# Rolling the first head into loops on VectorE and ScalarE, and VectorE's later heads into nested loops

## Chip, cores, metric

One core of one Trainium2 chip. The metric is the device time of the kernel in microseconds (us), as the median of several runs. Where a ratio is given, it is the mean time of one kernel's runs over that of the other's of the same rounds (for the experiments it comes out when the run that was profiled is left out), so it is not quite the ratio of the medians that are quoted beside it.

## The reference, cut to what matters

A decode step for one token: attention over a long key-value cache, a small feed-forward part, and sums.

```python
B, Sq, D = 1, 1, 448
Hq, Hkv, Sk, Dh = 16, 8, 65536, 256
q = (x @ wq) ...                        # one token, 16 query heads, two per cache head
scores = q @ k^T * Dh ** -0.5           # k_cache, v_cache: 8 x 65536 x 256 bf16
p = softmax(scores); o = p @ v; attn = o @ wo
y = (silu(x @ w_gate) * (x @ w_up)) @ w_down * sigmoid(x @ w_r)
out = x + attn + xn + y
```

The two caches are 537 MB, and every byte is used once.

## The kernel before

Each cache head is cut into U = 4 units. A unit has 4 MB of K twice and 4 MB of V twice, which pass through a ring of four 4 MB slots. For K, TensorE transposes (as f32 pairs), VectorE evicts (copies out) three of four PSUM tiles and ScalarE one; then TensorE forms the scores. Sixteen such transposes with their scores are called a set. Part A is the first head's K, part B runs 28 turns with one head's V beside the next head's K, part C is the last head's V.

The loads are issued by SyncE in one straight sequence. A load waits until its slot is free; a V pair (8 MB, one load) waits for two slots:

```python
def pair_item(u):
    ...
    item(("v", u), [(ap..., A_v_cache[0, h]...[:, n0:n0 + 2 * CH, :], "slot%d" % s)],
         [("FREE", r + i - NSLOT) for i in range(2)])      # both slots must be free
# [cut]
for t in range(NT):
    slot_item("k", t + U, 0)
    pair_item(t)
    if t % U == 0:
        item(("wo", t // U), ...)
    slot_item("k", t + U, 1)
```

What each engine loops over is a table; the rest is unrolled:

```python
LOOPS = {"pe": {"A": 2, "B": 1, "C": 2}, "dve": {"B": U}, "act": {"B": U}}
```

TensorE (`pe`) thus already loops over pairs of units in A. VectorE (`dve`) and ScalarE (`act`) have A unrolled, and a loop of four turns in B.

## Time and profile before

| | before |
|---|---|
| first three runs | 1280.39, 1280.41, 1281.96 us |
| profiled span | 1279.0 us |
| busy: TensorE, VectorE, ScalarE | 77%, 46%, 36% |
| DMA | 549.0 MB, 429 GB/s, 99.7% of 16 engines |

From the profile's page of the kernel before: the head, the busy times (with share of the span and count), the DMA row of 40 slices, and the queue table:

```profile
span 1279.0 us, 23059 instructions
PE 984.8 (77%) x9859; PEld 674.4 (53%) x9859; DVE 584.2 (46%) x1091; ACT 459.6 (36%) x655; POOL 4.6 (0%) x35
DMA  9999999999999999999999999999999999999998
...
q1 hardware_dynamic: 18322, 549.04, 99.7%
...
q14 instruction: 6, 0.05, 0.0%
```

The DMA engines are the bound. No compute engine is near its limit, and the DMA row has no gap. The question for any change to compute is therefore only whether a load is issued later than the moment its queue runs dry.

The timeline around the end of the first pass of A (start, duration, engine, line, instruction; in brackets the idle time before and what ended it):

```profile
77.77 0.26 PE L372 MATMUL ps_s<-sel_bf,s 128*128 128x8 bf16 x4 [0.71 <-ACT s L450]
78.06 0.42 DVE L474 CAST S_sb<-ps_s 128x256 bf16<-128x256 f32 x1 [2.15 <-PE ps_s L372]
78.52 0.42 DVE L476 TENSOR_REDUCE m1p<-S_sb 128x2 f32<-128x256 bf16 x1
78.60 3.71 PE L372 MATMUL ps_t<-ident_f,ring 128*128 128x128 f32 x32 [0.58 <-issue]
79.70 3.68 DVE L426 COPY kt_buf<-ps_t 128x1024 bf16<-128x1024 bf16 x6 [0.77 <-PE ps_t L372]
```

The two loads, from SyncE's timeline, and the short chain ahead of the second one:

```profile
107.65 0.33 SPq L826 DMA_DIRECT2D ring<-in_A_v_cache_dram  x1
...
1231.79 2.01 SPq L826 DMA_DIRECT2D ring<-in_A_v_cache_dram  x2
```

```profile
1210.26 0.40 DVE L474 CAST S_sb<-ps_s 128x256 bf16<-128x256 f32 x1
1210.69 0.42 DVE L476 TENSOR_REDUCE m1p<-S_sb 128x2 f32<-128x256 bf16 x1
1211.15 0.16 DVE L480 TENSOR_REDUCE m<-m1p 128x2 f32<-128x8 f32 x1
1211.84 0.28 DVE L488 TENSOR_REDUCE gmax<-ps_m 2x1 f32<-2x128 f32 x1 [0.53 <-PE ps_o L372]
```

The first V pair starts to move at about 109.6 us, the late one at about 1233.6 us (counting bytes of packets in order), so both are issued only about 2 us ahead. Most other loads are issued 5 to 17 us ahead. I call these two the tight hand-overs.

### The profile page before, as it was taken

The numbers are of one execution on the slowest core, as the hardware profiler recorded it, in microseconds if no ns is written. First come the engines' busy times: TensorE is split into PE (matmuls) and PEld (weight loads), VectorE is DVE, ScalarE is ACT, GpSimd is POOL, SyncE is SP. The second block draws the span as 40 slices with busy tenths as digits, with TensorE's granted clock in tenths as the row PEclk, the third lists the DMA queues.
The fourth block names the chain that finished last, engine by engine and source line by source line (L and its number), as shares of the span: only waits on it lengthen the run. The fifth ranks groups of instructions, "written<-read, shape, count | busy, mean of one in ns | idle before, by whom it ended". The sixth has DMA issues, their size and how long they took to land.

```text
span 1279.0 us, 23059 instructions
## 1 busy us (share of the span) xinstructions
PE 984.8 (77%) x9859; PEld 674.4 (53%) x9859; DVE 584.2 (46%) x1091; ACT 459.6 (36%) x655; POOL 4.6 (0%) x35
## 2 busy tenths in 40 slices
PE   4998877778777787677786777877787876888754
PEld 3877554555554564445554545644455544556421
DVE  2676544454444554344543445543355443555310
ACT  1555433353333543234432244432334333344210
POOL 1000000000000000000000000000000000000000
PEclk9998888897878998888988889988799788899885
DMA  9999999999999999999999999999999999999998
GB/s 409 427 426 432 434 430 422 436 427 446 430 429 430 428 446 430 435 423 428 439 438 432 430 425 436 439 435 430 424 435 430 445 430 424 432 431 442 425 437 346
DMA packets 18342, 549.22 MB, mean 429 GB/s; under 512 B 1942, under 2 KB 3992, under 8 KB 5144
## 3 DMA queue, kind: packets, MB, share of 16 engines
q1 hardware_dynamic: 18322, 549.04, 99.7%
q8 instruction: 8, 0.13, 0.0%
q14 instruction: 6, 0.05, 0.0%
q10 hardware_dynamic: 6, 0.00, 0.0%
HBM read 549.03 MB, written 0.00 MB: 429 GB/s over the span
## 4 chain that ended last, share of the span: by engine, by line
DMA 65%; PE 33%; issue 1%; DVE 0%; SPq 0%; ACT 0%; ACTq 0%
DMA ring<-in_A_k_cache_dram 59%; PE ps_t L372 24%; PE ps_q L372 6%; DMA ring<-in_A_v_cache_dram 5%; PE ps_m L372 2%; PE ps_s L372 1%; DMA wr_row<-in_B_w_r_dram 0%; SPq L826 0%; ACT s L450 0%; DVE rowsf L340 0%; DVE xe_row L335 0%; DVE stat L312 0%; DVE rowsf L342 0%; DVE rowsf L319 0%; ACTq L826 0%
## 5 line engine op out<-in xcount | busy, mean ns | idle before, releaser
L372 PE MATMUL ps_t<-ident_f,ring 128*128 128x128 f32 x4096 | 546.7, 288 | 103.4 <-DMA ring<-in_A_k_cache_dram 82.6
L426 DVE COPY kt_buf<-ps_t 128x1024 bf16<-128x1024 bf16 x768 | 488.1, 684 | 268.0 <-PE ps_t L372 267.5
L372 PEld LDWEIGHTS ps_t<-ident_f,ring 128*128 128x128 f32 x4096 | 474.0, 147 | 211.3 <-issue 103.2
L428 ACT ACTIVATE kt_buf<-ps_t 128x1024 bf16<-128x1024 bf16 x256 | 262.2, 1024 | 242.8 <-PE ps_t L372 242.7
L372 PE MATMUL ps_o<-ring,p_sb 128*4 128x512 bf16 x2040 | 193.1, 545 | 144.5 <-DMA ring<-in_A_v_cache_dram 144.4
L450 ACT ACTIVATE s<-ps_q 98x512 bf16<-98x512 f32 x256 | 152.9, 597 | 273.5 <-PE ps_q L372 273.5
L372 PEld LDWEIGHTS ps_o<-ring,p_sb 128*4 128x4 bf16 x2040 | 55.7, 106 | 252.2 <-issue 233.5
L372 PE MATMUL ps_q<-kt_buf,q_cur 128*2 128x512 bf16 x2048 | 164.4, 398 | 0.0
L517 ACT ACTIVATE p_sb<-S_sb 128x128 bf16<-128x128 bf16 x64 | 19.0, 309 | 252.2 <-PE ps_o L372 249.2
L532 DVE RECIPROCAL rs<-ps_m 128x4 f32<-128x4 f32 x29 | 5.3, 182 | 226.5 <-PE ps_m L372 226.5
L372 PEld LDWEIGHTS ps_s<-sel_bf,s 128*128 128x128 bf16 x1024 | 59.9, 98 | 53.8 <-ACT s L450 50.8
L372 PE MATMUL ps_s<-sel_bf,s 128*128 128x8 bf16 x1024 | 63.9, 168 | 22.6 <-ACT s L450 22.6
L568 DVE CAST ob_sb<-ps_o 100x512 bf16<-100x512 f32 x29 | 20.1, 692 | 117.2 <-PE ps_o L372 117.2
L605 DVE TENSOR_TENSOR rowsf<-ps_m,rowsf 1x448 f32<-1x448 f32 x28 | 17.1, 612 | 53.9 <-PE ps_m L372 53.9
L372 PEld LDWEIGHTS ps_m<-rowsum,ones_f 128*128 128x128 f32 x116 | 21.6, 262 | 22.3 <-issue 22.3
L372 PEld LDWEIGHTS ps_q<-kt_buf,q_cur 128*2 128x2 bf16 x2048 | 27.1, 79 | 10.2 <-issue 5.0
L372 PE MATMUL ps_m<-wo_cur,oT_sb 128*1 128x448 bf16 x112 | 25.7, 352 | 0.0
L372 PE MATMUL ps_m<-rowsum,ones_f 128*128 128x2 f32 x116 | 24.0, 312 | 0.0
L372 PE MATMUL ps_m<-xnT_sb,w_area 128*128 x112 | 14.7, 184 | 2.8 <-issue 2.8
L372 PEld LDWEIGHTS ps_m<-wo_cur,oT_sb 128*1 128x1 bf16 x112 | 9.3, 83 | 13.5 <-issue 0.9
L474 DVE CAST S_sb<-ps_s 128x256 bf16<-128x256 f32 x32 | 12.9, 404 | 4.3 <-PE ps_s L372 4.3
L372 PEld LDWEIGHTS ps_m<-xnT_sb,w_area 128*128 x112 | 11.7, 104 | 5.8 <-issue 3.3
(87 smaller groups left out, 161.7 us busy)
## 6 DMA issues: line engine op xcount, KB each, us to landing
ring<-in_A_k_cache_dram SPq DMA_DIRECT2D x64, 4096.0 KB, 26.4
ring<-in_A_v_cache_dram SPq DMA_DIRECT2D x2, 4096.0 KB, 31.1
ring<-in_A_v_cache_dram SPq DMA_DIRECT2D x2, 2048.0 KB, 28.9
w_area<-in_A_wq_dram SPq DMA_DIRECT2D x1, 3584.0 KB, 11.2
wo_cur<-in_A_wo_dram SPq DMA_DIRECT2D x7, 448.0 KB, 17.4
ring<-in_A_v_cache_dram SPq DMA_DIRECT2D x2, 1024.0 KB, 31.0
w_area<-in_B_w_gate_dram SPq DMA_DIRECT2D x1, 1568.0 KB, 24.0
w_area<-in_B_w_up_dram SPq DMA_DIRECT2D x1, 1568.0 KB, 27.4
```

The source lines that it names most:

```text
L372: return pe.matmul(*a, **k)
L426: O(e, ("EV", s, m), lambda it: nc.vector.tensor_copy(out=kt[:, :], in_=tb[:, :]), f"ev{m}")
L428: O(e, ("EV", s, m), lambda it: nc.scalar.activation(out=kt[:, :], in_=tb[:, :], func=ACTF.Copy), f"ev{m}")
L450: O("act", ("EVQ", s), lambda it: nc.scalar.activation(out=s2[s % 2][0:QROWS, :], in_=ps_q[0:QROWS, :], func=ACTF.Copy), "evq")
L474: O("dve", ("SCOPY", u), lambda it: nc.vector.tensor_copy(out=S, in_=ps_sn))
L517: O("act", ("PC", t, c), lambda it: nc.scalar.activation(out=p_sb[:, c, :, :], in_=S_sb[:, n:n + CH, :], func=ACTF.Copy), "pc")
L532: O("dve", ("RS", t), lambda it: nc.vector.reciprocal(out=rs[:, :, :], in_=ps_m[0:P, C_TOT:C_TOT + NH * rep]))
L568: O("dve", ("OB", t), lambda it: nc.vector.tensor_copy(out=ob_sb[0:OROWS, :], in_=ps_o[0:OROWS, :]))
L605: O("dve", ("RES", t), lambda it: nc.vector.tensor_tensor(out=base_f, in0=ps_m[0:1, C_BIG:C_BIG + D], in1=base_f, op=ALU.add))
```

## The change

The intent is smaller code with the same work in the same order: A becomes two passes on VectorE and ScalarE, and VectorE's B becomes one turn in two nested loops. To make one body serve all turns, addresses of the score copy and its maximum are computed from the loop counter, the maximum over units runs in every unit, and m1p is zeroed first.

```diff
-    LOOPS = {"pe": {"A": 2, "B": 1, "C": 2}, "dve": {"B": U}, "act": {"B": U}}
+    LOOPS = {"pe": {"A": 2, "B": 1, "C": 2}, "dve": {"A": 2, "B": (1, U)}, "act": {"A": 2, "B": U}}
 # [cut]
+        O("pool", "z_m1p", lambda it: v.memset(m1p[:, :, :], 0.0))
 # [cut]
+        W("dve", "z_m1p")
 # [cut: the start of the query projection becomes an operation of its own, semaphore counts]
-        S = S_sb[:, k * SBN:(k + 1) * SBN, :]
-        O("dve", ("SCOPY", u), lambda it: nc.vector.tensor_copy(out=S, in_=ps_sn))
+        if u < U:
+            at = lambda it, n: bass.ds(it * (2 * n) + (u % 2) * n, n)
+        else:
+            at = lambda it, n: bass.ds(it * n, n)
+        O("dve", ("SCOPY", u), lambda it: nc.vector.tensor_copy(out=S_sb[:, at(it, SBN), :], in_=ps_sn))
 # [cut: SMAX likewise]
-        if u >= U - 1:
-            W("dve", "SMAX", u)
-            W("dve", "M1T", u - 1)
-            O("dve", ("M1", u), lambda it: nc.vector.tensor_reduce(out=m1[:, :], in_=m1p[:, :, 0:k + 1], axis=AX.X, op=ALU.max))
+        W("dve", "SMAX", u)
+        W("dve", "M1T", u - 1)
+        O("dve", ("M1", u), lambda it: nc.vector.tensor_reduce(out=m1[:, :], in_=m1p[:, :, :], axis=AX.X, op=ALU.max))
 # [cut]
-        W("dve", "EXP", h - 1, rep - 1)
 # [cut: the loop emitter learns nested loops]
+            with eng.Fori(0, n // inner) as it:
+                if inner == 1:
+                    turn(it)
+                else:
+                    with eng.Fori(0, inner) as k:
+                        turn(k)
```

More of the change, by code (lines that the diff above doesn't have):

```diff
@@ L387, in pe_setup @@
         W_item("pe", "wq")
+        O("pe", "QT_START", lambda it: mm(ps_m[0:P, C_Q:C_Q + NH * rep], lhsT=ident_bf[:, :], rhs=zero_bf[:, 0:NH * rep], start=True, stop=False,
+                                          skip_group_check=True), "jt", 2)
         def qt(it):
             half = Hq * NH // 2
-            mm(ps_m[0:P, C_Q:C_Q + NH * rep], lhsT=ident_bf[:, :], rhs=zero_bf[:, 0:NH * rep], start=True, stop=False, skip_group_check=True)
             for n, c0, z0 in ((NE, 0, 0), (NE - 1, half, 2 * NE)):
@@ L400, in qt @@
             return mm(ps_m[0:P, C_Q:C_Q + NH * rep], lhsT=ident_bf[:, :], rhs=zero_bf[:, 0:NH * rep], start=False, stop=True, skip_group_check=True)
-        O("pe", "QT", qt)
+        O("pe", "QT", qt, "qk", 2)
         W("pe", "PSQ_ZERO")
@@ L469, in dve_scopy @@
     def dve_scopy(u):
-        k = u % U
         W("dve", "JT", u * SETS + SETS - 1)
         W("dve", "PC", u - U, HC - 1)
-        S = S_sb[:, k * SBN:(k + 1) * SBN, :]
-        O("dve", ("SCOPY", u), lambda it: nc.vector.tensor_copy(out=S, in_=ps_sn))
-        W("dve", "SCOPY", u)
-        O("dve", ("SMAX", u), lambda it: nc.vector.tensor_reduce(out=m1p[:, :, k], in_=S.rearrange("p n i -> p i n"), axis=AX.X, op=ALU.max))
-        if u >= U - 1:
-            W("dve", "SMAX", u)
-            W("dve", "M1T", u - 1)
-            O("dve", ("M1", u), lambda it: nc.vector.tensor_reduce(out=m1[:, :], in_=m1p[:, :, 0:k + 1], axis=AX.X, op=ALU.max))
+        if u < U:
[3 more added lines that the diff above has]
+        O("dve", ("SCOPY", u), lambda it: nc.vector.tensor_copy(out=S_sb[:, at(it, SBN), :], in_=ps_sn))
+        W("dve", "SCOPY", u)
+        O("dve", ("SMAX", u), lambda it: nc.vector.tensor_reduce(
+            out=m1p[:, :, at(it, 1)], in_=S_sb[:, at(it, SBN), :].rearrange("p n i -> p i n"), axis=AX.X, op=ALU.max))
+        W("dve", "SMAX", u)
+        W("dve", "M1T", u - 1)
+        O("dve", ("M1", u), lambda it: nc.vector.tensor_reduce(out=m1[:, :], in_=m1p[:, :, :], axis=AX.X, op=ALU.max))
     def pe_m1t(b):
@@ L826, in do, with loop @@
                 eng.dma_start(fn[0], fn[1]).then_inc(sems[sem], 16)
-        def loop(body, period):
+        def loop(body, period, inner=1):
             its = {}
@@ L858, in loop @@
                 assert all(v is None or v[0] == sem for v in vals), (e, rows[1][j], vals)
-                assert all(nums[i] == nums[0] + i * step for i in range(n)), (e, rows[1][j], nums)
+                per = 1
+                if inner > 1 and any(nums[i] != nums[0] + i * step for i in range(n)):
+                    per, step = inner, nums[inner] - nums[0]
+                assert all(nums[i] == nums[0] + i // per * step for i in range(n)), (e, rows[1][j], nums)
                 assert nums[0] >= 1 and step >= 0, (e, rows[1][j], nums)
@@ L867, in loop @@
                     continue
-                if period > 1 and step % period == 0 and nums[0] - sub[j] * (step // period) >= 1:
+                if per > 1:
+                    rk = (nums[0], step, None)
+                elif period > 1 and step % period == 0 and nums[0] - sub[j] * (step // period) >= 1:
                     rk = (nums[0] - sub[j] * (step // period), step // period, True)
@@ L879, in loop, with turn @@
             waited.clear()
-            with eng.Fori(0, n) as it:
+            def turn(it):
                 for j, (kind, lab, key, fn, sem) in enumerate(rows[0]):
@@ L889, in loop @@
                         for rk, r in regs.items():
-                            if rk[2] or j + 1 == len(sub):
+                            if rk[2] or rk[2] is False and j + 1 == len(sub):
                                 eng.reg_add(r, r, rk[1])
+            with eng.Fori(0, n // inner) as it:
[4 more added lines that the diff above has]
+                        turn(k)
+                    for rk, r in regs.items():
+                        if rk[2] is None:
+                            eng.reg_add(r, r, rk[1])
             waited.clear()
@@ L901, in emit @@
                     k2 += 1
-                loop(entries[k:k2], period)
+                loop(entries[k:k2], *(period if isinstance(period, tuple) else (period,)))
                 k = k2
```

## The prediction

> **What bounds the kernel now.** The 16 DMA engines. The page's head and queue table: one queue moves 549.0 MB in a 1279.0 us span, 429 GB/s, 99.7% of 16 engines' span; the DMA row shows 9 until the last slice. [...] Counting packets in flight, the engines are occupied from 1.9 to 1274.7 us without a hole; only head and a 4.3 us tail are without loads. PE is 77% busy, VectorE 46%, ScalarE 36%.
>
> **What the change does.** It shrinks code. The first head's unrolled code on VectorE (96 evictions) and ScalarE becomes two passes over two units; VectorE's later heads become one turn inside nested loops. Order of work per engine is the same; no load, matmul or eviction goes. Added:
> - a GpSimd memset (0.1 us) that VectorE waits for at 0.9 us; it then idles 4.0 us for the input row anyway;
> - three max reductions (0.16 us each) in the first head;
> - computed addresses for the score copy and its max, register additions, a back edge each turn. PE's own back edge at 78 us shows 0.6 us of idle; I take at most 0.5 us per VectorE back edge (estimate from that).
>
> Removed: one wait per turn and some instruction fetches (their queues carry 0.18 MB in 14 packets; a 16 KB packet took 1.1 us of one engine). TensorE keeps its 186 rows in order.
>
> **How much is critical.** Only what delays a load's issue past the moment its queue runs dry. By issue times against the start of each load's first packet (bytes counted in order), most loads are issued 5 to 17 us early. Two hand-overs are tight: the first V pair (issued 107.65 us, starts about 109.6) and a V pair near the end (issued 1231.79, starts about 1233.6). At both the mean number of busy DMA engines dips to 14.4 of 16 for about 1.5 us, so a delay there costs its full length.
> - The first is reached by TensorE's transposes at 2.53 us a set; the timeline shows VectorE idle 0.65 us and ScalarE 0.94 us in each. Later heads, already looped, keep 2.53 us too, so register waits fit. At the back edge (78 us) VectorE's first eviction may slip 0.3 us; PE needs that buffer about 0.5 us later. I expect 0, at most 0.5 us.
> - At the second, loop exit, addresses and the chain copy, max, M1 (1210.3 to 1211.3 us) may add 0.1 to 0.3 us.
> - Between, 28 back edges of at most 0.5 us (14 us of VectorE's time) fall into leads of 5 us or more and are not seen.
> - Fewer fetches give back perhaps 0.1 us.
>
> **Prediction.** 1280.5 us, 8 in 10 between 1279.4 and 1282.2 (before: 1280.39 to 1281.96). Faster by over 2%: 0.01. Within 2%: 0.98. Slower: 0.01.
>
> **Signs.** DMA at 99.7% and about 429 GB/s; first V pair issued at 107.6 to 108.2 us; first head at 2.53 us a set; 32 small max reductions; VectorE busy up by about 0.5 us; no more instruction packets than before; tail near 4 us.
>
> **What would make it wrong.** [...] If the first head runs slower than 2.53 us a set, the loss appears one for one at the first V pair.

## More of the kernel before

A pass of part A covers two units and ends with a drain, in which TensorE waits for ScalarE between short groups:

```python
def turn_A(u):
    ...
    for c in range(HC):
        k_slots(sets_of(u, c), first)
    if u % 2:
        n = (u + 1) * SETS
        k_JT(n - 2); k_QK(n - 1); k_JT(n - 1)
```

The 32 transposes that open the second pass took 3.71 us, and VectorE's first eviction began 1.10 us after them.

## The result, and the profile after

| | before | after |
|---|---|---|
| runs | 6 | 6 |
| median (range), us | 1280.77 (1280.39 to 1281.96) | 1281.94 (1281.06 to 1282.43) |
| ratio, 95% interval | | 1.0008, 0.9995 to 1.0020 |
| profiled span | 1279.0 us | 1280.5 us |
| VectorE busy, instructions | 584.2 us, 1091 | 585.1 us, 1094 |

The medians differ by 1.2 us and the spans by 1.5 us, and this is the question: is that the change, or something else? The same lines of the changed kernel:

```profile
span 1280.5 us, 23236 instructions
PE 993.4 (78%) x9859; PEld 678.6 (53%) x9859; DVE 585.1 (46%) x1094; ACT 459.1 (36%) x655; POOL 4.6 (0%) x36
...
q1 hardware_dynamic: 18322, 549.04, 99.7%
...
q14 instruction: 5, 0.04, 0.0%
```

```profile
77.87 5.35 PE L374 MATMUL ps_t<-ident_f,ring 128*128 128x128 f32 x32 [0.51 <-issue]
...
79.44 1.30 DVE L430 COPY kt_buf<-ps_t 128x1024 bf16<-128x1024 bf16 x2 [0.72 <-PE ps_t L374]
```

```profile
108.56 0.33 SPq L831 DMA_DIRECT2D ring<-in_A_v_cache_dram  x1
...
1234.78 0.33 SPq L831 DMA_DIRECT2D ring<-in_A_v_cache_dram  x1
```

```profile
1213.02 0.40 DVE L480 CAST S_sb<-ps_s 128x256 f32 x1
1213.57 0.42 DVE L482 TENSOR_REDUCE m1p<-S_sb  x1
1214.02 0.16 DVE L486 TENSOR_REDUCE m<-m1p 128x2 f32<-128x8 f32 x1
1214.89 0.28 DVE L494 TENSOR_REDUCE gmax<-ps_m 2x1 f32<-2x128 f32 x1 [0.71 <-PE ps_o L374]
```

Three things are to be seen. The 32 transposes took 1.64 us longer, although TensorE's code is the same. The first V pair was issued 0.91 us later and the late one 2.99 us later. And the chain of copy, maxima and gmax near the end, from the start of the copy to the start of gmax, grew from 1.58 to 1.87 us: 0.12 us ahead of the first maximum and 0.18 us ahead of gmax.

The start of each load's first packet shows where the time went: up to the first V pair the two traces agree within about 0.3 us; all later loads of part B start 0.7 to 1.2 us later, without growing; from the late V pair on they start 2.0 to 2.9 us later, and the end gives about 0.8 us back. The losses enter at the two tight hand-overs. The 2.99 us by which the late V pair was issued later add up so: TensorE began on the last K load 1.14 us later (inherited from the first hand-over), its first 16 transposes took 3.58 us in place of 1.97 us, and the chain took 0.29 us more.

The table of windows gives TensorE's granted clock, PEclk, as the third number from the end, here for 79 to 83 us, first before, then after (columns: window, length, busy time of PE, PEld, DVE, ACT and POOL with counts, then PEclk, DMA share, GB/s):

```profile
...
79.00:81.00 2.00, 2.00 (x21) 1.96 (x19) 1.29 (x3) 1.02 (x1) 0.00 (x0) 1.00 1.18 508
81.00:83.00 2.00, 2.00 (x23) 1.37 (x21) 2.00 (x4) 1.10 (x2) 0.00 (x0) 1.00 0.84 360
```

```profile
...
79.00:81.00 2.00, 2.00 (x11) 2.00 (x10) 1.40 (x3) 0.56 (x1) 0.00 (x0) 0.50 1.10 475
81.00:83.00 2.00, 2.00 (x16) 1.98 (x14) 1.21 (x3) 1.02 (x1) 0.00 (x0) 0.75 0.95 410
```

In the profile after, TensorE ran at half clock just here. The raw clock records put it at 0.5 from 78.57 to 81.98 us: 3.41 us. Stretches of 6.83 us at 0.5 elsewhere in the same records are twice that length. In the 3.41 us before the drop TensorE was busy for 1.80 us (more of this under r11).

**Two theories.** The *loop theory*: the added loop work on VectorE and ScalarE delays the hand-overs. The *clock theory*: TensorE's clock is at half rate at the hand-overs in some executions and not in others, in both kernels, and the first profiles happened to differ.

To measure what a hand-over costs I counted DMA packets in flight in each trace and integrated how far the count falls below 16, over 16 (the "hole", in us of all engines). Before: 0.14 us at the first hand-over, 0.10 us at the second. After: 0.46 and 1.18 us. A hole tells that a hand-over came late, but at the first one it understates the loss: moving from 40 to 60 MB took 47.1 us before and 48.0 us after, against 46.2 to 46.7 us in the five later profiles without a hole there (r4, r9 to r12).

### The profile page after: what moved, and what is told of

Its sections match the earlier page's. It is cut to its first block, busy times and chain, and to the rows that moved or that the text cites. A ratio compares the mean times of both kernels' runs of the same rounds, so it can differ in the third digit from the quotient of the medians.

```text
span 1280.5 us, 23236 instructions
## 1 busy us (share of the span) xinstructions
PE 993.4 (78%) x9859; PEld 678.6 (53%) x9859; DVE 585.1 (46%) x1094; ACT 459.1 (36%) x655; POOL 4.6 (0%) x36
## 2 busy tenths in 40 slices
DMA packets 18341, 549.21 MB, mean 429 GB/s; under 512 B 1942, under 2 KB 3992, under 8 KB 5144
## 3 DMA queue, kind: packets, MB, share of 16 engines
q1 hardware_dynamic: 18322, 549.04, 99.7%
## 4 chain that ended last, share of the span: by engine, by line
DMA 62%; PE 35%; issue 1%; DVE 1%; ACT 0%; SPq 0%; DVEq 0%; ACTq 0%
DMA ring<-in_A_k_cache_dram 59%; PE ps_t L374 26%; PE ps_q L374 6%; DMA ring<-in_A_v_cache_dram 3%; PE ps_m L374 2%; PE ps_s L374 1%; PE ps_o L374 1%; DMA wr_row<-in_B_w_r_dram 0%; ACT s L454 0%; SPq L831 0%; DVE kt_buf L643 0%; DVE rowsf L745 0%; DVE rowsf L342 0%; DVE stat L314 0%; DVE xe_row L337 0%
## 5 line engine op out<-in xcount | busy, mean ns | idle before, releaser
L374 PE MATMUL ps_t<-ident_f,ring 128*128 128x128 f32 x4096 | 563.6, 292 | 115.4 <-DMA ring<-in_A_k_cache_dram 91.9
L374 PEld LDWEIGHTS ps_t<-ident_f,ring 128*128 128x128 f32 x4096 | 479.8, 149 | 237.0 <-DMA ring<-in_A_k_cache_dram 111.5
L374 PE MATMUL ps_o<-ring,p_sb 128*4 128x512 bf16 x2040 | 182.3, 521 | 125.8 <-DMA ring<-in_A_v_cache_dram 125.7
L482 DVE TENSOR_REDUCE m1p<-S_sb x32 | 13.5, 422 | 4.5
L480 DVE CAST S_sb<-ps_s 128x256 f32 x32 | 12.9, 404 | 4.5 <-PE ps_s L374 4.5
```

What stands on the lines that cost most here:

```text
L374: return pe.matmul(*a, **k)
L480: O("dve", ("SCOPY", u), lambda it: nc.vector.tensor_copy(out=S_sb[:, at(it, SBN), :], in_=ps_sn))
L482: O("dve", ("SMAX", u), lambda it: nc.vector.tensor_reduce(out=m1p[:, :, at(it, 1)], in_=S_sb[:, at(it, SBN), :].rearrange("p n i -> p i n ...
```

## The experiments

### The two kernels again (r1, r2)

No edit.

> The kernel before, unchanged, timed against itself: a null. Ratio 1.0000 within 0.0007 by every theory. What it tells apart: by the clock theory (the 1 us between the kernels comes from where TensorE runs at half rate near the two tight hand-overs, a matter of phase) its profile may show another state than the first profile did: 32 transposes at the back edge of the first head (about 78 us) taking 5.3 us in place of 3.7 us, and then the first V pair issued about 1 us later (108.5 us), in this kernel too. By the loop theory (the added loop work delays the hand-overs) it again shows 3.7 us and 107.7 us.

> The changed kernel again. By the loop theory: 1.0 us slower again (ratio 1.0006 to 1.0010), and the first V pair issued at 108.5 us again with VectorE late at the back edge. By the clock theory the profile may show 3.7 us for the 32 transposes at the back edge and a V pair at 107.5 us, and the ratio may be anything from 1.0000 to 1.0012.

Measured: r1 1281.85 us (5 runs, ratio 1.0001 to the kernel before, 0.9987 to 1.0015); r2 1281.33 us (ratio 0.9999, 0.9985 to 1.0012). The kernel before in the same rounds: 1281.49 us, 1280.47 to 1283.5 in 9 runs. From r1, the kernel before:

```profile
78.33 5.35 PE L372 MATMUL ps_t<-ident_f,ring 128*128 128x128 f32 x32 [0.58 <-issue]
...
109.04 0.33 SPq L826 DMA_DIRECT2D ring<-in_A_v_cache_dram  x1
...
1234.80 0.33 SPq L826 DMA_DIRECT2D ring<-in_A_v_cache_dram  x1
```

And from r2, the changed kernel:

```profile
78.42 4.17 PE L374 MATMUL ps_t<-ident_f,ring 128*128 128x128 f32 x32 [0.51 <-issue]
...
79.99 3.68 DVE L430 COPY kt_buf<-ps_t 128x1024 bf16<-128x1024 bf16 x6 [0.72 <-PE ps_t L374]
...
107.94 0.33 SPq L831 DMA_DIRECT2D ring<-in_A_v_cache_dram  x1
...
1232.51 2.01 SPq L831 DMA_DIRECT2D ring<-in_A_v_cache_dram  x2
```

The roles are swapped: now the unchanged kernel shows slow transposes, late V pairs and a span of 1280.5 us (holes 0.31 and 1.85 us), and the changed one 1279.0 us (holes 0.27 and 0.17 us). The loop theory as the cause of the 1.5 us falls. A small part of it stays: at full clock the transposes took 4.17 us, not 3.71 us, and VectorE's first eviction began 1.57 us after them, not 1.10 us (ScalarE's began 0.67 us after them in both). That is the work added on VectorE at this edge, and not the back edge alone. Counted from the start of the transposes, its maximum of the scores ended at 0.65 us in place of 0.34 us, the added maximum ended at 0.85 us, and 0.72 us of idle time follow, which r5 will show to be the length of a back edge. From these figures I estimate that the longer chain without the back edge (ready at 0.85 us), or the back edge behind the old chain (1.06 us), would have been hidden. At half clock both kernels take 5.35 us, so there it is hidden.

### Each part alone (r3, r4)

```diff
 # r3: first head looped, later heads as before
-"dve": {"A": 2, "B": (1, U)}, "act": {"A": 2, "B": U}
+"dve": {"A": 2, "B": U}, "act": {"A": 2, "B": U}      # and constant addresses in B
 # r4: later heads nested, first head as before
+"dve": {"B": (1, U)}, "act": {"B": U}                 # and constant addresses in A
```

> The changed kernel with VectorE's and ScalarE's first head looped, but VectorE's later heads unrolled over four turns as before. Loop theory: the part of the loss that comes from the first hand-over, about half of 1 us (ratio about 1.0004), stays; the copy, max, M1 chain before the end is as short as before (copy to max 0.43 us start to start, max start to M1 start 0.46 us) since its addresses are constants again. Clock theory: the ratio follows what the profile shows at the two hand-overs, not this edit.

> The changed kernel with the first head unrolled on VectorE and ScalarE as before, later heads nested on VectorE. Loop theory: the second hand-over's part: copy to max 0.55 us start to start, first max of M1T 0.2 us later, so 0.3 us later at the second hand-over, ratio about 1.0002 to 1.0005, and the first V pair at 107.7 us. Clock theory: again as the profile shows at the hand-overs.

(Both keep the added maximum in every unit and the zeroing.) Measured: r3 1281.44 us (ratio 0.9997, 0.9983 to 1.0010), r4 1281.38 us (ratio 0.9999, 0.9985 to 1.0013). Neither part costs anything that a run shows. Their profiles follow the clock: r3 had transposes of 5.35 us and holes of 0.43 and 0.74 us (span 1280.1 us); r4 5.17 us, no hole at the first hand-over since its pass had begun 1.2 us earlier, 0.60 us at the second (1278.4 us). The near-end chain does follow the edit. r3, with constant addresses, then r4, with computed ones:

```profile
1212.92 0.40 DVE L480 CAST S_sb<-ps_s 128x256 bf16<-128x256 f32 x1
1213.36 0.42 DVE L482 TENSOR_REDUCE m1p<-S_sb 128x2 f32<-128x256 bf16 x1
```

```profile
1210.81 0.40 DVE L480 CAST S_sb<-ps_s 128x256 f32 x1
1211.35 0.42 DVE L482 TENSOR_REDUCE m1p<-S_sb  x1
```

0.44 us against 0.54 us from start to start: the computed address costs 0.1 us on this chain.

### A large delay in every turn, or once at the end (r5, r6)

```diff
+    def dose(key):           # on VectorE, 24 x tensor_reduce(dum[:, i:i+1] <- ones_f), used by nobody
 # r5: in turn_B, before the turn's other work
+        dose(("DOSE", t))
 # r6: once, in middle(), before pe_m1t(NU - 1)
+        dose(("DOSE", 0))
```

> The changed kernel with 24 useless reductions of 128x128 f32 on VectorE (about 6 us together, estimate from the 0.28 us of the small max) put at the start of each of the 28 later turns: what a very slow back edge would cost, some 170 us of VectorE's time in all. Lead theory (of the prediction: most loads are issued 5 to 17 us before their queue runs dry): time within 1 us of the changed kernel's, DMA still 99.7%. Rival, that VectorE's turn is on the path: tens of us longer, up to 170 us.

> The changed kernel with the same 24 reductions (about 6 us) once, on VectorE after the last turn, before the last head's maximum. Lead theory with the tight second hand-over: the V pair near the end is issued about 5 to 5.5 us later (6 us less the 0.7 us that VectorE waits there anyway), and the time rises by as much, 5 us (ratio about 1.004). Rival, that a single delay of this size is taken up by later leads or by noise: within 1 us.

Measured: r5 1282.89 us (1279.99 to 1283.66, ratio 1.0007, 0.9991 to 1.0022), r6 1286.1 us (ratio 1.0032, 1.0016 to 1.0047). A dose took 4.73 us, not the 6 us that I had estimated. Two neighbouring turns of r5, then the end of r6:

```profile
549.90 0.16 DVE L487 TENSOR_REDUCE m<-m1p 128x2 f32<-128x8 f32 x1
550.77 4.73 DVE L492 TENSOR_REDUCE dum<-ones_f 128x1 f32<-128x128 f32 x24 [0.71 <-issue]
590.94 0.16 DVE L487 TENSOR_REDUCE m<-m1p 128x2 f32<-128x8 f32 x1
592.06 4.73 DVE L492 TENSOR_REDUCE dum<-ones_f 128x1 f32<-128x128 f32 x24 [0.96 <-issue]
```

```profile
1214.62 4.73 DVE L492 TENSOR_REDUCE dum<-ones_f 128x1 f32<-128x128 f32 x24 [0.71 <-issue]
1219.27 0.27 DVE L502 TENSOR_REDUCE gmax<-ps_m 2x1 f32<-2x128 f32 x1
...
1239.09 2.01 SPq L840 DMA_DIRECT2D ring<-in_A_v_cache_dram  x2
```

132.5 us of useless VectorE work in 28 turns cost about 1 us, at most 2.8 us by the interval (which includes zero). r5's trace shows one new hole, about 1.3 us at 139 to 144 us, where the kernel before has a lead of only about 6 us; the other turns took it all up. The same 4.73 us once at the second hand-over cost 4.1 us by the ratio (0.0032 of 1281.4; the interval is 2 to 6 us), with a hole of 6.0 us. So leads decide, as the prediction said.

r5 also gives what the prediction had only estimated, since its dose waits for no other engine: the back edge costs VectorE 0.71 us inside a head and 0.96 us between two heads where the outer loop turns; the first entry took 1.97 us. All 28 sum to 22.7 us.

### Taking away the tight hand-overs (r7, r8)

```diff
-    pair_item(t)                       # one load of 8 MB, both slots free
+    for c in range(HC):
+        slot_item("v", t, c)           # two loads of 4 MB, each when its slot is free
```

> The kernel before with each 8 MB V pair loaded as two 4 MB loads, each issued as soon as its own ring slot is free: this takes away both tight hand-overs (the first half is issued about 10 us earlier at the first, 1.8 us earlier at the second). Clock theory (the spread of about 2 us comes from half-rate TensorE phases that reach the DMA queue only through these two hand-overs): both holes shrink below 0.1 us in the profile whatever the transposes take, times 0.5 to 1.5 us lower in the median than the kernel before, and a smaller spread. Rival, that the spread comes from DMA itself: no change in median or spread.

> The changed kernel with the same two loads for each V pair. Clock theory: the same gain, and no difference from the other split kernel beyond 0.3 us. Rival, that the changed loops cost something anywhere else than at the hand-overs: this stays about 1 us slower than the other split kernel.

Measured: r7 1282.91 us (1282.78 to 1283.12), r8 1281.94 us (1281.74 to 1282.41); the kernel before in the same rounds 1281.41 us (1280.38 to 1282.77). The transposes took 5.35 us in both profiles, yet both holes were gone (below 0.06 us). The spread fell from 2.4 us to 0.3 and 0.7 us. This half of the clock theory is shown: the spread enters through the hand-overs. The other half of my expectation failed: the times did not fall. What changed with the split is the number of packets:

```profile
DMA packets 22662, 549.22 MB, mean 429 GB/s; under 512 B 2422, under 2 KB 4472, under 8 KB 5624
```

That is r7's line; the kernel before moved the same bytes in 18,342 packets. V rows of 64 KB became rows of 32 KB, and the packets under 512 B rose too, from 1,942 to 2,422, 16 for each of 30 more loads. From 60 MB moved to 500 MB moved, all 12 profiles with whole V pairs in part B took 1017.0 to 1017.3 us, r7 1019.4 and r8 1019.2 us: about 2 us more. Whether the shorter rows or the additional loads cost it, no run tells apart.

### Closing them without splitting every pair (r9, r10)

```diff
 # the second feed-forward weights, 1.6 MB, move from unit 1 of the first head to just ahead of the first V pair
-            item("wd", [...])
 ...
         slot_item("k", t + U, 0)
+        if t == 0:
+            item("wd", [...])
         pair_item(t)
 # in part C only:
-            pair_item(t)
+            for c in range(HC):
+                slot_item("v", t, c)
```

> The kernel before with the second feed-forward weights (1.6 MB, about 3.7 us of DMA) loaded just ahead of the first V pair in place of 50 us earlier, and only the two V pairs of the last head split into two loads. The V pairs of the other heads stay whole, so the packets stay near 18,400 (22,662 when all were split). Theory (the hand-over holes cost 0.2 to 2 us and splitting every pair costs about 1.4 us through its packets): both holes below 0.1 us, time about 1280.2 us, spread under 1 us, 0.5 to 1.5 us below the kernel before. Rival (something else in the split kernels made them slow): again near 1282 us.

> The same two edits on the changed kernel. Theory: same time as the other filled kernel within 0.4 us, spread under 1 us: what is left of the change's effect once the hand-overs have leads is nothing. Rival, that its loops cost elsewhere: slower than the other by over 0.5 us in medians with spreads that do not overlap.

Measured: r9 1280.61 us (1280.36 to 1281.09), r10 1280.09 us (1279.47 to 1280.38); the kernel before in the same rounds 1281.53 us (1280.49 to 1282.41). Ratios 0.9994 (0.9980 to 1.0008) and 0.9990 (0.9977 to 1.0004). Holes at the hand-overs 0.05 us or less in both, with 5.35 us of transposes in both. So the holes go as expected, and the medians fell by 0.9 and 1.4 us against the kernel before, though the intervals include 1. The changed kernel was not the slower one here; its fill was 0.6 us faster in the mean, as r8 was 0.9 us faster than r7. I expected 0.3 to 0.4 us at most, and this is left open (below).

### Keeping TensorE busy in the drain (r11, r12)

```diff
+    def warm(key):      # two useless matmuls, 128x128 f32
+        O("pe", key, lambda it: [mm(ps_m[0:P, C_BIG:C_BIG + P], lhsT=ones_f[:, :], rhs=ident_f[:, :], start=True, stop=True) for _ in range(2)][-1])
     if u % 2:
         n = (u + 1) * SETS
-        k_JT(n - 2); k_QK(n - 1); k_JT(n - 1)
+        warm(...); k_JT(n - 2); k_QK(n - 1); warm(...); k_JT(n - 1); warm(...)
```

r11 is the changed kernel with this edit, r12 has r10's edits too.

> The changed kernel with two useless 128x128 f32 matmuls on TensorE (about 0.6 us) in each of the three idle gaps at the end of each pass over the first head (about 75 to 78 us), so that it is not idle there. Clock theory: the 32 transposes after the back edge take 3.7 us, not 5.3 us (5.35 in six of eight profiles of kernels with this edge as it was), and the first V pair is issued at about 107.3 to 108 us, after the pass is lengthened by at most 0.5 us by the fillers. Rival, that slow transposes there come from late evictions on VectorE: 5.3 us again. The time may not show it beyond noise: 0 to 1 us lower than the changed kernel.

> The changed kernel with both the fill of r10 and the fillers of r11. Theory (TensorE's slow phase in the first head costs time only through the tight first hand-over): where that hand-over has a lead already, warming adds nothing, so the time is that of r10 within 0.5 us (1280.1 us), though the 32 transposes take about 4.2 us. Rival (the fillers help somewhere else): 1279.5 us or less.

(The count is off: of all ten earlier kernels and the first two profiles, 5.35 us was seen in nine of the twelve, 5.17, 4.17 and 3.71 us once each.)

Measured: r11 1279.98 us (1279.41 to 1280.56, 4 runs; ratio 0.9990, 0.9975 to 1.0006); r12 1279.96 us (1279.81 to 1280.14; ratio 0.9992, 0.9978 to 1.0006). From r11:

```profile
76.14 0.71 PE L374 MATMUL ps_m<-ident_f,ones_f 128*128 128x128 f32 x4
...
77.03 0.69 PE L374 MATMUL ps_m<-ident_f,ones_f 128*128 128x128 f32 x4
77.70 4.16 PE L374 MATMUL ps_t<-ident_f,ring 128*128 128x128 f32 x32
...
107.20 0.33 SPq L838 DMA_DIRECT2D ring<-in_A_v_cache_dram  x1
```

With the drain filled the clock records stay at 1.0 through the edge in r11 and r12, and the transposes took 4.16 and 4.15 us. I had written 3.7 us, overlooking VectorE's back edge, which r2 had already shown to make it 4.17 us. Filling the drain gives what the fill of the queue gives, and both together give no more, so I find no cost of the slow transposes except through the first hand-over. (In r11's profile the second hand-over happened to have no hole either.)

Why do some executions keep the clock without fillers? In each trace all clock records begin on one grid of 3.413 us (within 2 ns), and where the grid lies over the drain differs from execution to execution. Call one step of this grid a window. The window that ended at the drop held 1.40 to 1.95 us of busy TensorE in the ten profiles that lost the clock. The window at the same place held 2.02 and 2.12 us in the two unfilled ones that kept it (r2, first before), 3.28 and 3.35 us in r11 and r12. Nothing suggests that the kernel decides it: with VectorE's first head unrolled, four of five unfilled profiles lost the clock, with it looped, six of seven. So r11 is the test: its transposes began 3.25 us after that window's start, and all ten unfilled profiles in which they began 2.57 us or more after it lost the clock. r12 alone proves nothing: there they began 2.17 us after it, as in the first profile before, which kept the clock unfilled. Busy time alone gives no rule for the whole trace: elsewhere windows with 1.4 us kept the clock and some with 2.1 us lost it (the first profile after has both, 1.43 and 2.11 us).

Across all 12 profiles with a whole first V pair (eight are listed) one sum holds: from the start of the 32 transposes to the issue of the first V pair it is 25.3 us plus what the transposes took.

| profile | kernel | transposes start, us | they take | first V pair issued | holes, us | span, us |
|---|---|---|---|---|---|---|
| first | before | 78.60 | 3.71 | 107.65 | 0.14, 0.10 | 1279.0 |
| first | after | 77.87 | 5.35 | 108.56 | 0.46, 1.18 | 1280.5 |
| r1 | before | 78.33 | 5.35 | 109.04 | 0.31, 1.85 | 1280.5 |
| r2 | after | 78.42 | 4.17 | 107.94 | 0.27, 0.17 | 1279.0 |
| r3 | first head only | 78.40 | 5.35 | 109.09 | 0.43, 0.74 | 1280.1 |
| r4 | nested only | 77.20 | 5.17 | 107.72 | none, 0.60 | 1278.4 |
| r10 | after, filled | 77.66 | 5.35 | 108.35 | none, none | 1277.7 |
| r11 | after, warmed | 77.70 | 4.16 | 107.20 | none, none | 1277.6 |

## Why the prediction was right

- *The bound.* The predicted range of 1279.4 to 1282.2 us held the measured 1281.94 us. That says little by itself: the runs of the unchanged kernel alone went from 1280.3 to 1283.5 us, wider than this range, and two of the six runs behind the median lay above it. DMA stayed at 99.7%, and r5 showed that 132 us more of VectorE work in the turns costs about 1 us. That the turns have long leads is shown.
- *Only the hand-overs count.* Shown: the difference of the first two traces enters there, 4.73 us put at the second one costs 4.1 us, and with both closed the spread shrinks (r7 to r10, r12).
- *The first hand-over: "I expect 0, at most 0.5 us".* The loop's own part is 0.46 us at full clock (4.17 less 3.71 us) and nothing at half clock (5.35 us in both kernels). It came at the upper end. The slip of VectorE's eviction was 0.47 us, not 0.3 us. The profile's line names TensorE as the releaser of a wait of 0.72 us here; but that wait has the same 0.71 us that r5 shows for a back edge with nothing to wait for, so it is probably the back edge. The prediction had also said that TensorE needs that buffer about 0.5 us later, which should have hidden such a slip. That held for the first buffer only: in the first profile before, the next two were freed 0.28 and 0.12 us ahead of the transposes that reuse them, since VectorE frees one in 0.60 us and TensorE fills one in 0.44 us.
- *The second: "0.1 to 0.3 us".* Measured 0.29 us in the first profile after (1.87 less 1.58 us). About 0.1 us of it is the computed address (r3 against r4).
- *"At most 0.5 us per VectorE back edge".* Too small: 0.71 to 0.96 us, 22.7 us in all and not 14. The conclusion did not depend on it.
- *Signs.* VectorE's busy time rose by 0.9 us, not 0.5 us. The first V pair was to be issued at 107.6 to 108.2 us. It was at 108.56 us in the profile and at 107.94 us in the next one. The step that failed is "First head at 2.53 us a set": the first pair of sets after the edge ran at half clock. I had read the clock off one profile, that of the kernel before, as if it belonged to the kernel. It belongs to the execution: the same kernel's transposes took 3.71 us in its first profile and 5.35 us in r1. So the slow hand-overs were not foreseen, and that the median stayed in the range in spite of them was partly luck.
- *"Fewer fetches give back perhaps 0.1 us".* Instruction packets went from 14 to 13. No run shows a gain that can be laid to it.

**What the change costs.** Eleven runs of the changed kernel (first six, r2) have a mean of 1281.66 us, forty-seven of the kernel before (first six, all control runs, r1) 1281.35 us; they spread over 2.4 and 3.2 us. The difference of 0.3 us has a standard error of about 0.25 us. By my estimate from the traces it should be 0.3 to 0.8 us where the hand-overs are tight and zero where they are not, which is within what these means allow.

**What stays open.** The changed kernel was 0.9 us faster than the other where every pair was split (r8, r7) and 0.6 us where the queue was filled (r10, r9). In the profiles, 0.2 to 0.4 us of it lies in when the last bytes start, about 0.7 us in how long they take from there to TensorE's last V matmuls, and in r10 another 0.36 us in closing matmuls that took 0.55 in place of 0.91 us. The time from last bytes to last V matmuls also swings within one kernel: 1.0 and 0.2 us in the first profile before and r1, 0.3 and 1.1 us in the first after and r2. What sets it, no run told apart, and so a small gain from the change at the tail is not ruled out. The versions r10, r11 and r12 had lower medians than both kernels, by 1.0 to 2.0 us; their intervals against the kernel before include 1, so that gain is not shown by them alone.

## What to carry to other kernels

In a kernel bound by DMA, as this one is at 99.7%, ask of a compute change only which loads it issues later, and how long before its queue runs dry each load is issued: here 132.5 us of extra VectorE work in turns with long leads cost about 1 us (r5), while 4.73 us at the tight hand-over cost 4.1 us (r6). Before explaining a difference of 0.1%, run the unchanged kernel again with a profile: here the second profile of the same kernel showed the very signature (transposes of 5.35 us, late V pairs, r1) that one was about to lay to the change. A load that nobody needs for long, moved ahead of the tight hand-over, closed the first hole here (0.05 us or less, r9 and r10) at no cost that a run showed; cutting all V loads in two closed the holes too (below 0.06 us, r7 and r8), but moving from 60 to 500 MB took about 2 us more.

## What else the traces show of TensorE's clock

- A drop came after short gaps. The drain has gaps of 0.7, 0.7 and 0.5 to 0.6 us in the twelve profiles without fillers, and in ten of them the clock fell to 0.5 after it. With these gaps filled it stayed at 1.0 in both profiles (r11; r12 alone proves nothing, as said above). In the ten that lost it, the window of 3.41 us that ended at the drop held 1.40 to 1.95 us of busy TensorE; this is no rule, as said under r11.
- After longer waits the pace varied too: where TensorE had idled 1.6 to 2.5 us before the last K load, 16 transposes took 1.97 to 2.40 us in five profiles; where it had idled 3.6 us or more, 2.90 to 3.67 us in nine.
- Transposes alone did not keep the clock from rising again: in the first profile after, the window at half clock from 78.57 to 81.98 us held nothing but transposes, and the clock was 1.0 right after it. 32 transposes took 3.71 us at full clock (the first profile before) against 5.35 us where most of them ran at half clock (the first profile after).
